# Mode rows in five kinds, turns rounded in bf16, and magnitude products issued twice

## The chip, the cores and the metric

One core of one Trainium2 chip runs the whole program. The metric is the device time of one execution in microseconds (us). The engines are named as the profile names them: PE is TensorE, PEld its weight loads, DVE is VectorE, ACT is ScalarE, POOL is GpSimd, SP is SyncE, which issues most DMAs.

## The reference

Four layers act on a 2048 x 512 sequence: A, B, A, B, each added to its input after a layer norm.

```
x = A_q
x = x + _A_ref(_layernorm(x), A_k, A_v, A_shift_k, A_ssm_k, A_ssm_D)
x = x + _B_ref(_layernorm(x), B_log_A_real, B_A_imag, B_C_real, B_C_imag, B_log_dt, B_D_skip)
(the same two lines again)

_A_ref: kv = (4-tap causal conv of k) * v;  q * (causal conv of kv with ssm_k + kv * ssm_D)
_B_ref: A = -exp(log_A_real) + i A_imag;  C = (C_real + i C_imag) * dt;  dt = exp(log_dt)
        P = exp(A * dt * pos)                       (512 channels, 128 modes, 2048 positions)
        K = 2 * Re(sum over modes of C * P);        causal conv of u with K, + u * D_skip
```

The part that the change touches makes K. For each channel and mode it needs a magnitude, exp(rate * n) with an offset log|C|, and an angle, rate * n with an offset arg C. Angles are counted in turns, and only their fraction matters for sine and cosine.

## The kernel before

The long convolutions are done by Fourier transforms built from matmuls, in chunks: `fwd_group` (L175, matmuls on L173, first step), `f2_chunk` (L195, matmul on L198, second step), a product with a spectrum on POOL and DVE (L285 to L288), and the way back (L297, L318). Constants of these steps are `wz`, `w2`, `mm`, `w4`.

The program has these stages. First, DVE, ACT and POOL prepare the mode numbers from the inputs (L342 to L433). The rates and offsets (four arrays of 128 x 512) go through `split` (L366), which cuts a float into three bf16 pieces: ACT copies to bf16 (L370, L372), POOL or DVE subtracts (L371, L373), and SP writes the pieces to a scratch array `rows_d` in DRAM (L374). Then two generators run side by side, one turn of the first to two of the second (`run_steps`):

- `stream`, with `taps` in it, makes K in 64 units of 8 channels, four units to a group `gi`. `load_rows` (L474) fetches a group's rows from DRAM into a tile `rw`, of which three exist. `mags` (L482) is a bf16 matmul of the rows with a table (`tg1` or `tg2`) into a PSUM bank, and then an exp on ACT (L492). `exps` does this for two groups at a time, 12 tiles, ahead of every eighth unit: a burst. `angles` (L497) multiplies rows with the table `tt` (L501), rounds the turns to a whole number `y` on DVE (L505) and subtracts it in PSUM with a second matmul by `minus`, the negated identity (L506). `waves` takes sine and cosine on ACT (L512 to L514), `products` multiplies with the magnitudes on POOL and DVE (L524 to L528), `contract` sums over the modes on PE (L538). All of `mags` and `angles` share three PSUM banks, tag `pa`.
- `diagonal` makes the spectrum of layer A's kernel (`spectrum_quarter`, L225; its tiles are `kk`, `pc`, `spec`) and the product kv (`gated`, L629), and then runs the first A convolution.

After that come the first gated update (L755), the B convolution, and both once more. A timeline planner orders the instructions of each engine ahead of time, by its own costs; on the chip every engine runs its list in order. So other instructions in `mags` and `angles` also change the order of the work around them.

In the kernel before, a row tile `rw` has 128 rows: two halves of 64 rows for two sets of 8 channels; each half has rates and offsets of 8 channels, in three pieces and a row of zeros. The tables `tt` and `tg1` are used with one half alone (the slice `hs`, 64 rows), `tg2` with all 128 rows. Turns reach some 1000, so `y` and `minus` are `F32R`, a float type for which the matmul loads its own weights: the program holds no separate weight load for it.

Of the kernel before, what the change touches and what calls it, by code (L numbers as in the profile page):

```python
# [79 lines left out]
def mode_constants():  # L80
    m = np.arange(32)
    n2 = np.concatenate([32 + m, 31 - m])
    tabs = {
        "tt": (8, np.concatenate([m + 1, 64 * m + 32]), np.repeat([0, 1], 32)),
        "tg1": (8, n2, 0 * n2),
        "tg2": (16, 64 * m, 0 * m + 1),
    }
    out = {}
    for name, (chans, rate, off) in tabs.items():
        t = np.zeros((2, 2, 8, 4, chans, len(rate)), np.float32)  # L90
        for s in range(2):
            for c in range(8):
                for r, factors in enumerate((rate, off)):
                    t[s, r, c, :3, (8 * s + c) % chans] = factors
        out[name] = t.reshape(128, chans, len(rate))
    out["minus"] = -np.eye(128, dtype=np.float32)
    return out

# [2 lines left out]
def kernel(ctx: ExitStack, tc: tile.TileContext, out, x_in, kv_in, ssmk_in, ssmd_in,  # L101
                           la_in, ai_in, cr_in, ci_in, ldt_in, ldtb_in, dsk_in,
                           w1_in, w2_in, mm_in, w4_in, minus_in, tt_in, tg1_in, tg2_in, dbg=None):
    nc = tc.nc
    V, S, G, T = nc.vector, nc.scalar, nc.gpsimd, nc.tensor
# [11 lines left out]
    kdram = [dram.tile([128, 512], F32, name=f"kdram{g}") for g in range(16)]  # L117
    ya_d = dram.tile([4, 128, 16, 128], F32, name="ya_d")
    kv_d = [dram.tile([128, 512], F32, name=f"kv_d{g}") for g in range(16)]
    rows_d = [dram.tile([NQ, 2, 128, 4, 128], BF16, name=f"rows_d{k}") for k in range(2)]  # L120

    cpool = sbuf(ctx, "cpool")
    GL = 2
# [230 lines left out]
    halfpi = gp.tile([128, 1], F32, name="halfpi")  # L354
    G.memset(halfpi, math.pi / 2)

    minus = gp.tile([128, 128], F32R, name="minus")
    G.dma_start(minus, minus_in)

    pieces = []  # L360
    for i in range(4):
        parts = nat.tile([128, 4, 4, 128], BF16, name=f"parts{i}")
        G.memset(parts[:, 3], 0.0)
        pieces.append(parts)

    def split(i, v, eng):  # L366
        k, r = divmod(i, 2)
        parts = pieces[i]
# [5 lines left out]
        nc.sync.dma_start(rows_d[k].rearrange("q h (s r c p) g n -> r (q h s) c (p g n)", s=2, r=2, p=4)[r],  # L374
                          parts.rearrange("p s g n -> p (s g n)"))

    bits = lambda t_: t_.bitcast(I32)
# [20 lines left out]
    split(2, la, G)  # L398
    y0 = nat.tile([128, 4, 128], F32, name="y0", tag="y0")
    V.tensor_scalar(y0, ai, MAGIC, MAGIC, op0=ALU.add, op1=ALU.subtract)  # L400
# [20 lines left out]
    V.tensor_mul(ph, ph, t0)  # L421
    V.scalar_tensor_tensor(ph, ph, -0.125, cr, op0=ALU.add, op1=ALU.mult)
# [44 lines left out]


    NR = 3
    rows, ms, pks, angs = {}, {}, {}, {}  # L470
    NM = 5
    last_exp, last_sin = [None], [None]

    def load_rows(gi):  # L474
        if gi in rows:
            return
        rows[gi] = wk.tile([128, 2, 2, 128], BF16, name="rw", tag="rw", bufs=NR)
        q, g = divmod(gi, 4)
        for k in range(2):
            nc.sync.dma_start(rows[gi][:, k], rows_d[k][q, :, :, g, :].rearrange("h x n -> x h n"))  # L480

    def mags(gi, k, col):  # L482
        h, s = divmod(k, 2)
        hs = slice(0, 128) if col == 2 else slice(64 * s, 64 * s + 64)
        pm = pp.tile([128, 512], F32, name="pm", tag="pa", bufs=NPA)
        T.matmul(pm, rows[gi][hs, 1, h, :], tabs["tg2" if col == 2 else "tg1"][hs], start=True, stop=True)  # L486
# [5 lines left out]
        i = S.activation(m, pm.rearrange("p (c i) -> p c i", c=16 if col == 2 else 8), AF.Exp)  # L492
        if last_sin[0] is not None:
            after(i, last_sin[0])
        last_exp[0] = i

    def angles(gi, k):  # L497
        h, s = divmod(k, 2)
        hs = slice(64 * s, 64 * s + 64)
        pa = pp.tile([128, 512], F32, name="pa", tag="pa", bufs=NPA)  # L500
        T.matmul(pa, rows[gi][hs, 0, h, :], tabs["tt"][hs], start=True, stop=False,  # L501
                 skip_group_check=True)

        y = wk.tile([128, 512], F32R, name="y", tag="y", bufs=2)
        V.tensor_scalar(y, pa, MAGIC, MAGIC, op0=ALU.add, op1=ALU.subtract)  # L505
        T.matmul(pa, minus, y, start=False, stop=True, skip_group_check=True)  # L506
        angs[gi, k] = pa
# [465 lines left out]
```

## Time and profile before

| what | value |
|---|---|
| median of three runs | 729.88 us (729.4 to 730.36) |
| profiled execution, its own time | 731.89 us |
| its span in the profile | 730.1 us |
| mean granted TensorE clock | 0.921 |
| PE busy | 587.1 us (80%) |
| DVE / ACT / POOL busy | 525.5 / 487.2 / 461.7 us |

The profiled execution took 2.0 us more than the median. In rows of the profile, `out<-in` are tile names, a form such as `64*128 64x512 bf16` is weights of 64 rows by 128 columns and moving data of 64 rows by 512 columns, and `[t <-X]` says that the engine was idle for t us until X released it. A float32 matmul stands as two instructions, so `x8` on L198 is one chunk of four matmuls, `x4` in an order row. "PEclk" is the share of full TensorE clock that was granted.

### The profile page before, as it was taken

The page shows a single profiled execution, that of the slowest core. Times are in us where ns is not written, and L with a number is a line of the kernel's source. Part 1 is how long each engine was busy: PE and PEld are TensorE (multiplying, and loading weights), DVE is VectorE, ACT ScalarE, POOL GpSimd, SP SyncE. Part 2 cuts the span into 40 slices and gives each one's busy share as a digit, 9 for nine tenths or more (in the row PEclk, how much of TensorE's full clock was granted, in tenths as well). Part 3 has the DMA queues.
Part 4 walks back from the last instruction along what each step waited for, and adds up shares of the span by engine and source line. Part 5 has one row for each costly group of instructions (what it writes and reads, how often), then busy time and mean ns, then how long its engine had stood idle before and what let it go on. Part 6 is the DMA issues. An engine that isn't in the chain of part 4 may idle for free.

```text
span 730.1 us, 14266 instructions
## 1 busy us (share of the span) xinstructions
PE 587.1 (80%) x4984; PEld 398.4 (55%) x4984; DVE 525.5 (72%) x947; ACT 487.2 (67%) x886; POOL 461.7 (63%) x483
## 2 busy tenths in 40 slices
PE   1376677589899999988998886988699808889996
PEld 0043444346576876665755464866377503666683
DVE  8836869868585874663565879566498898988875
ACT  3355566468779786785799667987457356696672
POOL 5535978859958695594596532077567502786783
PEclk9998999957999999998999898999899958999998
DMA  8556967766776477554473495668776250477772
GB/s 289 188 165 213 320 210 244 215 199 212 226 224 168 128 177 202 152 154 144 131 232 109 141 333 183 209 155 218 182 202 188 62 148 0 116 191 211 195 226 101
DMA packets 84555, 134.47 MB, mean 184 GB/s; under 512 B 16764, under 2 KB 33924, under 8 KB 83332
## 3 DMA queue, kind: packets, MB, share of 16 engines
q1 hardware_dynamic: 83268, 131.01, 60.8%
q0 software_dynamic: 1216, 2.56, 1.5%
q8 instruction: 39, 0.64, 0.4%
q14 instruction: 32, 0.26, 0.1%
HBM read 98.28 MB, written 35.65 MB: 183 GB/s over the span
## 4 chain that ended last, share of the span: by engine, by line
PE 31%; DVE 9%; ACT 9%; issue 5%; POOL 3%; DMA 3%; SPq 0%; DVEq 0%; POOLq 0%; ACTq 0%
PE pu L198 9%; PE pf L173 7%; PE po L318 6%; PE pi L297 6%; DMA kab<-spec 3%; ACT u L818 2%; DVE x L755 1%; POOL sw L287 1%; DVE w L312 1%; PE pk L538 1%; DVE x L832 1%; DVE vv L285 1%; ACT sw L283 1%; PE pm L486 1%; ACT sw L284 1%
## 5 line engine op out<-in xcount | busy, mean ns | idle before, releaser
L287 POOL TENSOR_TENSOR sw<-sw,kab 128x512 f32<-128x512 f32 x96 | 125.4, 1312 | 82.9 <-ACT sw L284 65.4
L285 DVE TENSOR_TENSOR vv<-pu,kab 128x512 f32<-128x512 f32 x96 | 65.1, 681 | 73.9 <-ACT sw L284 40.7
L297 PE MATMUL pi<-vv,mm 128*128 128x128 f32 x768 | 106.0, 283 | 9.3 <-DVE vv L285 6.7
L297 PEld LDWEIGHTS pi<-vv,mm 128*128 128x128 f32 x768 | 95.8, 195 | 21.6 <-issue 14.2
L288 POOL TENSOR_TENSOR vv<-vv,sw 128x512 f32<-128x512 f32 x76 | 98.9, 1304 | 7.8 <-DVE vv L285 5.3
L283 ACT ACTIVATE sw<-pu 64x512 f32<-64x512 f32 x96 | 57.1, 595 | 59.7 <-PE pu L198 56.4
L173 PE MATMUL pf<-kk,wz 128*128 128x256 f32 (+1 forms) x176 | 61.9, 599 | 39.3 <-issue 16.0
L636 POOL TENSOR_TENSOR term<-kvt 128x512 f32<-128x512 f32 x64 | 81.8, 1298 | 17.6 <-ACT acc L642 13.6
L198 PE MATMUL pu<-x,w 128*128 128x128 f32 x512 | 80.3, 304 | 13.1 <-ACT pc L249 9.0
L524 POOL TENSOR_TENSOR xye<-co,m 128x512 f32<-128x512 f32 x64 | 75.3, 1177 | 18.2 <-ACT co L514 9.0
L198 PEld LDWEIGHTS pu<-x,w 128*128 128x128 f32 x512 | 72.0, 212 | 27.2 <-ACT pc L249 10.1
L198 PEld LDWEIGHTS pu<-zu,w 128*128 128x128 f32 x512 | 62.7, 191 | 41.0 <-DVE vv L285 14.7
L198 PE MATMUL pu<-zu,w 128*128 128x128 f32 x512 | 72.6, 284 | 10.3 <-DVE vv L285 8.3
L173 PE MATMUL pf<-u,wz 128*128 128x256 f32 (+2 forms) x280 | 77.5, 493 | 3.7 <-DVE zu L191 2.5
L492 ACT ACTIVATE m<-pm 128x512 f32<-128x512 f32 x96 | 52.7, 612 | 18.3 <-PE pm L486 17.4
L318 PE MATMUL po<-w,w 128*64 128x512 f32 x192 | 57.2, 683 | 9.5 <-DVE w L312 8.2
L512 ACT ACTIVATE co<-pa 128x512 f32<-128x512 f32 x64 | 38.5, 601 | 38.0 <-PE pa L506 32.2
L249 ACT COPY pc<-pu 128x512 f32<-128x512 f32 x64 | 36.7, 586 | 39.1 <-PE pu L198 15.5
L173 PEld LDWEIGHTS pf<-kk,wz 128*128 128x128 f32 (+1 forms) x176 | 29.1, 220 | 55.4 <-issue 40.2
L538 PEld LDWEIGHTS pk<-xye 128*32 128x32 f32 x2048 | 36.8, 116 | 37.0 <-issue 18.4
L538 PE MATMUL pk<-xye 128*32 128x64 f32 x2048 | 51.6, 235 | 6.3 <-DVE ks L548 4.0
L284 ACT COPY sw<-pu 64x512 f32<-64x512 f32 x96 | 55.5, 578 | 1.1
(141 smaller groups left out, 1118.8 us busy)
## 6 DMA issues: line engine op xcount, KB each, us to landing
kab<-spec SPq DMA_DIRECT2D x188, 256.0 KB, 4.1
spec<-pc SPq DMA_DIRECT2D x64, 256.0 KB, 2.8
kvt<-kv_in SPq DMA_DIRECT2D x16, 624.0 KB, 5.8
yaq<-ya_d SPq DMA_DIRECT2D x5, 1024.0 KB, 8.6
kk<-ssmk_in SPq DMA_DIRECT2D x16, 256.0 KB, 4.8
kv_d<-un SPq DMA_DIRECT2D x16, 256.0 KB, 3.1
xt<-x_in SPq DMA_DIRECT2D x16, 256.0 KB, 4.3
kdram<-ks SPq DMA_DIRECT2D x64, 64.0 KB, 3.1
```

The lines of the kernel that those rows point to most:

```text
L173: yield T.matmul(o, w, rhs, start=True, stop=True)
L198: ins = T.matmul(pu[:, i, :], w2[:, c * CK + i, :], z[:, :, c * CK + i, :], start=True, stop=True)
L283: S.mul(sw[0:64], pu[64:128], -1.0)
L284: swapped[0] = S.copy(sw[64:128], pu[0:64])
L285: multiplied[0] = V.tensor_mul(vv, pu, kabs[s][:, 0])
L287: (V if last else G).tensor_mul(sw, sw, kabs[s][:, 1])
L288: (V if last or s % add_dve == add_dve - 1 else G).tensor_add(vv, vv, sw)
L297: i1s[t] = T.matmul(pi[:, i, :], mm[:, c * CK + i, :], vvs[t][:, i, :], start=True, stop=True)
L318: ins = T.matmul(po[64 * a:64 * a + 64], w4, ws[g][:, :, 16 * a:16 * a + 16, :].rearrange("p x t r -> p t x r"), start=True, stop=True, ti ...
L524: G.tensor_mul(xye[:, 0, :, 32:96], co[:, :, 1:65], m[:, :, 32:96])
L538: T.matmul(pk[32 * i4:32 * i4 + 32, 2 * k + i, :], xye[:, r, 4 * i + i4, 64:96], xye[:, r, 4 * i + i4, 0:64], start=r == 0, stop=r == 1, t ...
L636: G.tensor_mul(term, kvt[:, 3 - j:19 - j, :], tap(j))
```

## The change

Four things change, and L numbers after the change are given where order rows show them.

1. A fifth kind of row is made: `y0`, the fraction of 32 times the turns per step (three DVE instructions), which goes through `split` like the others. The table `tt` now is (m + 1) times the first fraction, (2m + 1) times the second, plus the offset. Turns stay below some 50, so that a whole number of turns is exact in bf16.
2. `y` and `minus` are bf16. Their matmul now has a weight load of its own.
3. A row tile holds five kinds x 8 channels x 3 pieces = 120 rows for each of the four units of a group, fetched by one DMA (two before). Every matmul of `mags` and `angles` uses all 120 rows. A `tg2` tile, one matmul of 512 columns before, takes two of 256.
4. In groups 0 to 5 (`WG = 6`) every product of `mags` is issued twice, with the same result.

```
+    tabs = {
+        "tt": {0: np.concatenate([m + 1, none]), 1: np.concatenate([none, 2 * m + 1]),
+               2: np.repeat([0, 1], 32)},
+        "tg1": {3: n2},
+        "tg2": {3: 64 * m, 4: none + 1},
+    }
...
-    rows_d = [dram.tile([NQ, 2, 128, 4, 128], BF16, name=f"rows_d{k}") for k in range(2)]
+    rows_d = dram.tile([16, 5, 8, 3, 4, 128], BF16, name="rows_d")
...
-    minus = gp.tile([128, 128], F32R, name="minus")
+    minus = gp.tile([128, 128], BF16, name="minus")
...
-        parts = nat.tile([128, 4, 4, 128], BF16, name=f"parts{i}")
-        G.memset(parts[:, 3], 0.0)
...
+        parts = nat.tile([128, 3, 4, 128], BF16, name=f"parts{kind}")
...
+    V.tensor_scalar(y0, ai, 32.0, MAGIC, op0=ALU.mult, op1=ALU.add)
+    V.tensor_scalar(y0, y0, MAGIC, None, op0=ALU.subtract)
+    V.scalar_tensor_tensor(y0, ai, 32.0, y0, op0=ALU.mult, op1=ALU.subtract)
+    split(1, y0, G)
...
-        rows[gi] = wk.tile([128, 2, 2, 128], BF16, name="rw", tag="rw", bufs=NR)
-        for k in range(2):
-            nc.sync.dma_start(rows[gi][:, k], rows_d[k][q, :, :, g, :].rearrange("h x n -> x h n"))
+        rows[gi] = wk.tile([120, 4, 128], BF16, name="rw", tag="rw", bufs=NR)
+        nc.sync.dma_start(rows[gi], rows_d[4 * q:4 * q + 4, :, :, :, g, :].rearrange("k a c p n -> (a c p) k n"))
...
-        T.matmul(pm, rows[gi][hs, 1, h, :], tabs["tg2" if col == 2 else "tg1"][hs], start=True, stop=True)
+        if col == 2:
+            for i in (0, 1, 0, 1)[:4 if gi < WG else 2]:
+                T.matmul(pm[:, 256 * i:256 * i + 256], rows[gi][:, k + i, :], tabs["tg2"], start=True, stop=True)
+        else:
+            for _ in range(2 if gi < WG else 1):
+                T.matmul(pm, rows[gi][:, k, :], tabs["tg1"], start=True, stop=True)
...
-        T.matmul(pa, rows[gi][hs, 0, h, :], tabs["tt"][hs], start=True, stop=False,
+        T.matmul(pa, rows[gi][:, k, :], tabs["tt"], start=True, stop=False, skip_group_check=True)
...
-        y = wk.tile([128, 512], F32R, name="y", tag="y", bufs=2)
+        y = wk.tile([128, 512], BF16, name="y", tag="y", bufs=2)
```

The order moves at three places that matter below. The first is the start of PE's list, before the change (`tg_217` is the table `tg2`, `tg_219` is `tg1`, `w_104` is `w2`, `x` a spectrum tile):

```order
L173 MATMUL pf<-kk,wz 128x16x16x2 x8
L486 LDWEIGHTS rw
L486 MATMUL pm<-tg_217,rw 128x512
L486 LDWEIGHTS rw
L486 MATMUL pm<-tg_219,rw 128x512
L486 LDWEIGHTS rw
L486 MATMUL pm<-tg_219,rw 128x512
L198 MATMUL pu<-x,w_104 128x128 x8
```

And the same place after it (`tg_222` is `tg2`, `tg_224` is `tg1`; L174, L199, L485 and L488 are the lines L173, L198 and L486 of before):

```order
L174 MATMUL pf<-kk,wz 128x16x16x2 x8
L199 MATMUL pu<-x,w_103 128x128 x8
L174 MATMUL pf<-kk,wz 128x16x16x2 x2
L485 LDWEIGHTS rw
L485 MATMUL pm<-tg_222,rw 128x256
L485 LDWEIGHTS rw
L485 MATMUL pm<-tg_222,rw 128x256
L485 LDWEIGHTS rw
L485 MATMUL pm<-tg_222,rw 128x256
L485 LDWEIGHTS rw
L485 MATMUL pm<-tg_222,rw 128x256
L488 LDWEIGHTS rw
```

Two chunks of the A spectrum (L198, 8 matmuls) and a transform step now stand ahead of the first magnitudes, which are four short products where one long one stood.

The second place is DVE's list at the end of the preparation, before the change (`t_151` is log|C|, `parts` the pieces that are written to DRAM):

```order
L418 TENSOR_TENSOR t_151<-t_151,t_150 128x512
L422 SCALAR_TENSOR_TENSOR ph<-ph,cr 128x512
L423 SCALAR_TENSOR_TENSOR ph<-ph,ci 128x512
L191 STREAM_TRANSPOSE x<-pf 128x512 x2
L371 TENSOR_TENSOR rest<-ph,parts_143 128x512
L373 TENSOR_TENSOR parts_143<-rest,parts_143 128x512
L371 TENSOR_TENSOR rest<-t_151,parts_147 128x512
L373 TENSOR_TENSOR parts_147<-rest,parts_147 128x512
```

And after it (L398 to L400 are the new fraction, L192 is L191 of before, L365 and L367 are L371 and L373):

```order
L398 TENSOR_SCALAR y_168<-ai 128x512
L416 TENSOR_TENSOR t_142<-t_142,t_141 128x512
L420 SCALAR_TENSOR_TENSOR ph<-ph,cr 128x512
L399 TENSOR_SCALAR y_168<-y_168 128x512
L192 STREAM_TRANSPOSE x<-pf 128x512 x2
L421 SCALAR_TENSOR_TENSOR ph<-ph,ci 128x512
L400 SCALAR_TENSOR_TENSOR y_168<-ai,y_168 128x512
L365 TENSOR_TENSOR rest<-ph,parts_207 128x512
L192 STREAM_TRANSPOSE x<-pf 128x512 x2
L367 TENSOR_TENSOR parts_207<-rest,parts_207 128x512
L365 TENSOR_TENSOR rest<-t_142,parts_214 128x512
L367 TENSOR_TENSOR parts_214<-rest,parts_214 128x512
```

Three more instructions and a second pair of transposes now stand ahead of the last pieces.

The third place is PE's list in the stretch where taps, spectrum and A convolution run together, before the change:

```order
L297 MATMUL pi<-vv,mm 128x128 x4
L173 MATMUL pf<-u,wz 128x16x8x2 x4
L506 MATMUL pa<-y,minus 128x512 x2
L173 MATMUL pf<-kk,wz 128x16x8x2 x4
L198 MATMUL pu<-x,w_104 128x128 x4
L297 MATMUL pi<-vv,mm 128x128 x4
L506 MATMUL pa<-y,minus 128x512
L173 MATMUL pf<-u,wz 128x16x8x2 x2
```

And after it (L298 and L505 are L297 and L506 of before):

```order
L298 MATMUL pi<-vv,mm 128x128 x4
L174 MATMUL pf<-u,wz 128x16x8x2 x4
L505 LDWEIGHTS minus
L505 MATMUL pa<-y,minus 128x512
L505 LDWEIGHTS minus
L505 MATMUL pa<-y,minus 128x512
L174 MATMUL pf<-kk,wz 128x16x8x2 x4
L199 MATMUL pu<-x,w_103 128x128 x4
L298 MATMUL pi<-vv,mm 128x128 x4
L505 LDWEIGHTS minus
L505 MATMUL pa<-y,minus 128x512
L174 MATMUL pf<-u,wz 128x16x8x2 x2
```

The order is the same here; each subtraction of whole turns now has a weight load ahead of it.

More of the change, by code (lines that the diff above doesn't have):

```diff
@@ L82, in mode_constants @@
     n2 = np.concatenate([32 + m, 31 - m])
+    none = 0 * m
     tabs = {
-        "tt": (8, np.concatenate([m + 1, 64 * m + 32]), np.repeat([0, 1], 32)),
-        "tg1": (8, n2, 0 * n2),
-        "tg2": (16, 64 * m, 0 * m + 1),
+        "tt": {0: np.concatenate([m + 1, none]), 1: np.concatenate([none, 2 * m + 1]),
+               2: np.repeat([0, 1], 32)},
+        "tg1": {3: n2},
+        "tg2": {3: 64 * m, 4: none + 1},
     }
     out = {}
-    for name, (chans, rate, off) in tabs.items():
-        t = np.zeros((2, 2, 8, 4, chans, len(rate)), np.float32)
-        for s in range(2):
+    for name, kinds in tabs.items():
+        t = np.zeros((5, 8, 3, 8, len(kinds[max(kinds)])), np.float32)
+        for kind, factors in kinds.items():
             for c in range(8):
-                for r, factors in enumerate((rate, off)):
-                    t[s, r, c, :3, (8 * s + c) % chans] = factors
-        out[name] = t.reshape(128, chans, len(rate))
+                t[kind, c, :, c] = factors
+        out[name] = t.reshape(120, 8, -1)
     out["minus"] = -np.eye(128, dtype=np.float32)
@@ L355, with split @@
     G.memset(halfpi, math.pi / 2)
-    minus = gp.tile([128, 128], F32R, name="minus")
+    minus = gp.tile([128, 128], BF16, name="minus")
     G.dma_start(minus, minus_in)
-    pieces = []
-    for i in range(4):
-        parts = nat.tile([128, 4, 4, 128], BF16, name=f"parts{i}")
-        G.memset(parts[:, 3], 0.0)
[L364 to L368, printed above, removed]
+    def split(kind, v, eng):
+        parts = nat.tile([128, 3, 4, 128], BF16, name=f"parts{kind}")
         rest = nat.tile([128, 4, 128], F32, name="rest", tag="rest", bufs=2)
@@ L373, in split @@
         eng.tensor_sub(parts[:, 2], rest, parts[:, 1])
-        nc.sync.dma_start(rows_d[k].rearrange("q h (s r c p) g n -> r (q h s) c (p g n)", s=2, r=2, p=4)[r],
+        nc.sync.dma_start(rows_d[:, kind].rearrange("a c p g n -> a c (p g n)"),
                           parts.rearrange("p s g n -> p (s g n)"))
@@ L397 @@
     G.tensor_mul(la, la, across(dtn))
-    split(2, la, G)
+    split(3, la, G)
     y0 = nat.tile([128, 4, 128], F32, name="y0", tag="y0")
@@ L423 @@
     V.scalar_tensor_tensor(ph, ph, 0.25, ci, op0=ALU.add, op1=ALU.mult)
-    split(1, ph, V)
-    split(3, t2, V)
+    split(2, ph, V)
+    split(4, t2, V)
     S.activation(warm, t2[:, 0, 0:1], AF.Exp, scale=0.0)
     tabs = {}
-    for key, c_, w_, src in (("tg2", 16, 32, tg2_in), ("tg1", 8, 64, tg1_in), ("tt", 8, 64, tt_in)):
-        tabs[key] = gp.tile([128, c_, w_], BF16, name=key)
+    for key, w_, src in (("tg2", 32, tg2_in), ("tg1", 64, tg1_in), ("tt", 64, tt_in)):
+        tabs[key] = gp.tile([120, 8, w_], BF16, name=key)
         G.dma_start(tabs[key], src)
@@ L469 @@
     NR = 3
+    WG = 6
     rows, ms, pks, angs = {}, {}, {}, {}
@@ L476, in load_rows @@
             return
-        rows[gi] = wk.tile([128, 2, 2, 128], BF16, name="rw", tag="rw", bufs=NR)
+        rows[gi] = wk.tile([120, 4, 128], BF16, name="rw", tag="rw", bufs=NR)
         q, g = divmod(gi, 4)
-        for k in range(2):
-            nc.sync.dma_start(rows[gi][:, k], rows_d[k][q, :, :, g, :].rearrange("h x n -> x h n"))
+        nc.sync.dma_start(rows[gi], rows_d[4 * q:4 * q + 4, :, :, :, g, :].rearrange("k a c p n -> (a c p) k n"))
     def mags(gi, k, col):
         h, s = divmod(k, 2)
-        hs = slice(0, 128) if col == 2 else slice(64 * s, 64 * s + 64)
         pm = pp.tile([128, 512], F32, name="pm", tag="pa", bufs=NPA)
-        T.matmul(pm, rows[gi][hs, 1, h, :], tabs["tg2" if col == 2 else "tg1"][hs], start=True, stop=True)
+        if col == 2:
[4 more added lines that the diff above has]
+                T.matmul(pm, rows[gi][:, k, :], tabs["tg1"], start=True, stop=True)
         if col == 2:
@@ L497, in angles @@
     def angles(gi, k):
-        h, s = divmod(k, 2)
-        hs = slice(64 * s, 64 * s + 64)
         pa = pp.tile([128, 512], F32, name="pa", tag="pa", bufs=NPA)
-        T.matmul(pa, rows[gi][hs, 0, h, :], tabs["tt"][hs], start=True, stop=False,
-                 skip_group_check=True)
-        y = wk.tile([128, 512], F32R, name="y", tag="y", bufs=2)
+        T.matmul(pa, rows[gi][:, k, :], tabs["tt"], start=True, stop=False, skip_group_check=True)
+        y = wk.tile([128, 512], BF16, name="y", tag="y", bufs=2)
         V.tensor_scalar(y, pa, MAGIC, MAGIC, op0=ALU.add, op1=ALU.subtract)
```

## Prediction

> **What bounds the kernel now.** I read the page first for the balance of the engines, then the busy time by stage, then PE's instructions in order of time where the clock is low.
>
> ```profile
> span 730.1 us, 14266 instructions
> PE 587.1 (80%) x4984; PEld 398.4 (55%) x4984; DVE 525.5 (72%) x947; ACT 487.2 (67%) x886; POOL 461.7 (63%) x483
> core 0: us, PE busy (x) PEld busy (x) DVE busy (x) ACT busy (x) POOL busy (x), PEclk, DMA share, GB/s
> 41.00:59.00 18.00, 15.48 (x75) 9.33 (x75) 8.74 (x14) 10.29 (x19) 8.18 (x9) 1.00 0.59 193
> 59.00:65.90 6.90, 5.41 (x16) 3.49 (x17) 2.65 (x6) 1.74 (x3) 2.69 (x3) 0.51 0.17 47
> 65.90:144.40 78.50, 53.77 (x648) 32.59 (x646) 64.06 (x123) 46.31 (x82) 64.97 (x68) 0.93 0.79 254
> 144.40:158.00 13.60, 11.52 (x84) 6.24 (x85) 7.26 (x18) 8.36 (x14) 7.94 (x10) 0.50 0.84 259
> 158.00:161.40 3.40, 2.69 (x14) 0.81 (x14) 3.04 (x6) 3.04 (x6) 1.29 (x2) 1.00 0.26 91
> 161.40:171.70 10.30, 9.74 (x27) 5.49 (x25) 7.69 (x14) 8.29 (x15) 9.75 (x10) 0.50 0.72 232
> 171.70:225.00 53.30, 47.78 (x645) 34.64 (x644) 40.74 (x74) 42.49 (x77) 42.66 (x47) 1.00 0.66 201
> 225.00:300.00 75.00, 72.73 (x718) 52.78 (x718) 47.31 (x79) 58.20 (x100) 53.98 (x57) 1.00 0.66 171
> 300.00:425.00 125.00, 110.80 (x1200) 73.67 (x1198) 75.99 (x123) 95.86 (x167) 82.48 (x83) 0.92 0.55 158
> ```
>
> PE is the fullest engine, but not everywhere. From 65.9 to 144.4 it works 53.8 of 78.5 us; DVE, POOL and the transfers (0.79, 254 GB/s) are ahead of it, so PE work there has room. From 144.4 to 171.7 PE is nearly always busy, at half clock for two stretches of 13.6 and 10.3 us. From 225 to 300 it is 97% busy at full clock: there more PE work is more time. From 300 to 425 it has gaps again. After 425 the changed code hardly runs, and I take that part as only shifted.
>
> ```profile
> 145.47 2.08 PE L198 MATMUL pu<-x,w 128*128 128x128 f32 x8 [2.97 <-ACT pc L249]
> 150.68 2.07 PE L173 MATMUL pf<-kk,wz 64*128 64x512 f32 x2
> 152.68 1.15 PE L486 MATMUL pm<-tg,rw 128*128 128x512 bf16 x3
> 163.68 2.08 PE L198 MATMUL pu<-x,w 128*128 128x128 f32 x8
> 172.18 1.16 PE L198 MATMUL pu<-x,w 128*128 128x128 f32 x8
> 602.72 10.01 PE L767 MATMUL idle<-x,wz 128*128 128x512 f32 x16 [17.19 <-issue]
> 601.80:608.60 6.80, 5.88 (x7) 2.52 (x8) 6.80 (x22) 5.48 (x14) 0.00 (x0) 0.50 0.00 0
> 608.60:612.00 3.40, 3.40 (x9) 1.52 (x8) 2.99 (x22) 2.51 (x8) 0.50 (x1) 1.00 0.01 2
> ```
>
> The same chunk of L198 takes 2.08 us at half clock and 1.16 at full. What brings the clock back is not being busy alone. The idle matmuls of L767, full 128 x 128 weights, restored it after 5.88 us of work. In the low stretch, 11.52 busy us bring it back for one step of 3.4 us, and it falls again; there the transforms (L173) and most magnitude products fill 64 of the 128 rows.
>
> **The change part by part.** Sums are against the profiled execution's 731.9 us, which stands 2.0 above the median of 729.9; 2.0 comes off at the end.
>
> *Start.*
>
> ```profile
> 41.01 1.15 PE L486 MATMUL pm<-tg,rw 128*128 128x512 bf16 x3 [4.15 <-DMA rw<-rows_d]
> 42.09 3.60 PE L198 MATMUL pu<-x,w 128*128 128x128 f32 x16
> 60.49 2.08 PE L198 MATMUL pu<-x,w 128*128 128x128 f32 x8 [4.00 <-ACT pc L249]
> L400 DVE TENSOR_SCALAR y<-ai 128x512 f32<-128x512 f32 x1 | 0.4, 413 | 0.0
> L422 DVE SCALAR_TENSOR_TENSOR ph<-ph,cr 128x512 f32<-128x512 f32 x1 | 1.8, 1751 | 0.0
> L191 DVE STREAM_TRANSPOSE x<-pf 128x512 f32<-128x512 f32 x32 | 20.9, 690 | 5.8 <-PE pf L173 5.8
> ```
>
> The first magnitudes wait 4.15 us for their rows, and 3.60 us of transform work waits behind them. DVE gets two instructions like L400 (0.41 each), one like L422 (at most 1.75, priced at 1.2) and two transposes (0.69 each) ahead of the last pieces: 3.4 us. The last write is three quarters as large, which I put at 1 us back, so rows come some 2.3 us later. But the two chunks now run inside the wait, so PE's list starts about 2.8 us earlier and is not idle. The first burst gets 4.6 us longer (next part): PE is 1.9 us late at 56. There it waits 4.00 us for a copy that waits for a transfer, which takes up the 1.9. Net 0, between -2.8 and +4.6. The extra casts on ACT and two subtractions on POOL lie beside the DVE work; four POOL memsets and one row DMA of each group go, and no engine waits on those.
>
> *Doubled and split products.* The price of a bf16 product with its load, from a pair:
>
> ```profile
> 229.68 0.71 PE L486 MATMUL pm<-tg,rw 128*128 128x512 bf16 x2
> 230.32 0.94 PE L198 MATMUL pu<-x,w 128*128 128x128 f32 x6
> L486 PEld LDWEIGHTS <-rw 128*128 128x128 bf16 x20 | 2.0, 98 | 3.4 <-issue 2.8
> ```
>
> Two take 0.64, so 0.32 each; 0.10 of it is the load, 0.22 streaming. One of 256 columns is then 0.10 + 0.11 = 0.21. A group had 6 products, 1.92 us; a doubled one has 8 x 0.21 + 8 x 0.32 = 4.24. A burst of two groups is 4.6 us longer at full clock. Three bursts are doubled: the first is counted above; the second lies near 100 us, where PE has room (0, at most 4.6); the third in the low stretch, where PE is idle for 3.3 of 27.3 us. I let 1.5 of it vanish there and take +3.1.
>
> *Clock.* Full rows and doubled products are the kind of work that L767 shows to restore the clock. From 150.7 on, PE is at half clock and busy for 7.3 + 9.7 = 17.0 us; at full clock this saves 1 - 1.16 / 2.08 = 44%, or 7.5. The stretch at 59 to 65.9 (5.41 busy, worth 2.4) may close too, since the idle time ahead of it shrinks; I take half. Together -8.7, between -9.9 and 0.
>
> *Turns in bf16.* DVE's rounding reads the same PSUM bank and writes fewer bytes; I price it the same, 0.67. The product by `minus` on PE:
>
> ```profile
> 240.12 1.89 PE L173 MATMUL pf<-u,wz 128*128 128x256 f32 x8
> 241.66 0.82 PE L506 MATMUL pa<-y,minus 128*128 128x512 f32 x2
> 244.04 0.39 PE L198 MATMUL pu<-x,w 128*128 128x128 f32 x2
> 246.06 1.03 PE L173 MATMUL pf<-u,wz 128*128 128x256 f32 x4
> 247.02 0.39 PE L501 MATMUL pa<-tt,rw 64*128 64x512 bf16 x1
> 247.34 1.13 PE L173 MATMUL pf<-u,wz 128*128 128x256 f32 x4
> 248.40 0.39 PE L501 MATMUL pa<-tt,rw 64*128 64x512 bf16 x1
> L506 PEld LDWEIGHTS pa<-y,minus 128*128 128x128 f32 x45 | 8.2, 193 | 9.7 <-DVE y L505 7.0 <-DVE xye L526 0.8 <-issue 0.5
>   DVE y L505: 10.3, 12
> by line: issue 12.5%; PE pu L198 11.4%; PE pf L173 11.1%; PE po L318 6.5%; PE pi L297 5.8%; PE pk L538 4.9%; ACT m L492 4.2%; ACT co L512 4.0%; ACT co L514 3.5%; PE pm L486 3.5%; ACT x L298 3.1%; ACT L513 3.1%; DVE w L312 3.0%; POOL xye L52
> ```
>
> From 240.12 to 244.04 run sixteen L173 and two L506. Eight L173 without a neighbour take 1.73 (0.216 each), so the two L506 cost 3.92 - 3.46 = 0.46, or 0.23 each: their loads are hidden. From 246.06 to 248.40 eight L173 and one bf16 product take 2.34, 0.61 more; 0.10 of it is the next product's load. A lone bf16 product among float32 ones costs 0.51: its load and the load behind it both show. So the bf16 form is dearer by 0.28 alone, and by 0.09 beside another bf16 product (0.32). In the last 40 units the new order has 13 alone and 27 beside one: 3.6 + 2.4. Twenty split `tg2` tiles add 0.10 each, 2.1 in all: 8.1 us of PE work from 172 to 425. PE's share of the path there lies between the 97% busy up to 300 and the 43% that its lines have in the chain of waits after (the last row); 0.7 gives 5.7. Against it, 12 loads of `minus` waited for `y` in this stretch; a separate load need not, and saves 0.19 each on a path on which PE is awaited: -2.3. Net +3.4, between -2.8 and +8.1.
>
> Sum: 0 + 3.1 - 8.7 + 3.4 = -2.2; 731.9 - 2.2 - 2.0 = 727.7.
>
> **The rivals.**
>
> *The turns are paid in full.* The stretch up to 300 leaves no room, and the waits saved are none, because what ends last there is DVE. Then 8.1 stands for 3.4: 732.4. For it: 72.73 of 75.00 busy. Against it: PE idles 14 us from 300 to 425.
>
> *The low clock stays* (the slower side). PE reaches the third burst after a wait like the 2.97 us at 145.47, the clock drops, and work at half clock is too thin to restore it. Then -8.7 is lost and the burst costs 9.2 for 3.1: 742.5. It is decided by whether PE's idle time just ahead of the third burst stays over 3 us, and by whether the doubled products then restore the clock at all. The Trainium skill, "TensorE: Matmul & The Clock Gate", section "What's actually happening", has the array at full clock after one window of some 3.4 us in which PE was busy. By that rule alone fuller rows would change nothing, as PE was busy already, and this rival would hold; the 11.52 busy us at 0.50 speak against busy time as the whole measure, and I leave it a chance.
>
> *Loads run ahead.* If the load of `minus`, which never changes, slips under the matmul before it, a bf16 product costs 0.22, no more than the 0.23 of now, and the waits saved stay: -2.8 instead of +3.4, 721.5. The Trainium skill, same page, section "Step-by-step: what each phase is for", says that weight loads are pulled ahead of matmuls in flight where row groups differ or the spare weight buffer is free. Against it: rows of full and half height alike show 0.32 per bf16 product here, load and stream one after the other.
>
> *Transfers set the pace up to 172.* Clock and doubling are both hidden there: 731.9 + 3.4 - 2.0 = 733.3. For it: 0.79 to 0.84 DMA share. Against it: PE is busy without gaps from 150.7.
>
> **How the numbers follow.** A change under 0.2% (728.4 to 731.3) can't be told from none here. My forecast, 727.7, has a chance of 0.43, its own range 724 to 731 (faster 0.33, same 0.10). Turns in full 0.20 (slower 0.15, same 0.05), low clock 0.12 (slower), loads ahead 0.10 (faster), transfers 0.15 (slower 0.11, same 0.04). That makes faster 0.43, same 0.19, slower 0.38. The range 719 to 738 takes in all cases but the low clock, and the ends of the unknown terms.
>
> **What would show it.** Right: a PEclk of 0.8 or more between 140 and 175; PE already at work on L199 before 41 us; the chunk of L198 that starts at 172.18 starting some 5 us earlier. L505 products at 0.5 us among float32 ones, and PE over 97% busy from 220 to 300, would show the price of bf16. Wrong: half clock through the third burst, or a start of the first magnitudes later than 45 us with PE idle before it; or bf16 products at a pitch of 0.22.

## The result and the profile after

| | before | after |
|---|---|---|
| median of four runs beside each other | 729.64 us (722.87 to 730.36) | 705.85 us (699.70 to 707.13) |
| ratio, 95% interval | 1 | 0.9677 (0.9597 to 0.9758) |
| profiled execution, its span, granted clock | 731.89, 730.1 us, 0.921 | 707.13, 705.4 us, 0.939 |

The kernel is 3.2% faster. The forecast was 727.7 us with a range of 719 to 738: the sign was right, the size was not, and the time lies 13 us below the range. A run that took over 1.5% longer than the fastest of its kernel is left out of every ratio here and below, so a ratio is not always that of the medians beside it. Line numbers of the changed kernel are one more than before in the transforms (L199 is L198 of before) and one less in the products and behind them (L537 is L538, L641 is L642, L754 is L755); the exp of the magnitudes is L494, L492 before.

The busy line of the page after, with the same columns as before:

```profile
span 705.4 us, 14397 instructions
PE 574.8 (81%) x5060; PEld 401.1 (57%) x5064; DVE 523.1 (74%) x950; ACT 487.8 (69%) x888; POOL 460.3 (65%) x481
```

PE has 76 instructions more and is busy 12.3 us less. The busy time by stage, after, in the stretches that the prediction used:

```profile
core 0: us, PE busy (x) PEld busy (x) DVE busy (x) ACT busy (x) POOL busy (x), PEclk, DMA share, GB/s
59.00:65.90 6.90, 4.30 (x14) 1.53 (x15) 6.90 (x13) 4.90 (x8) 6.45 (x6) 0.83 0.97 339
65.90:144.40 78.50, 63.14 (x721) 36.98 (x724) 65.56 (x130) 49.37 (x87) 64.71 (x71) 0.85 0.76 253
144.40:158.00 13.60, 11.34 (x86) 6.86 (x79) 9.62 (x17) 9.38 (x17) 9.49 (x10) 0.96 0.67 223
161.40:171.70 10.30, 8.32 (x111) 6.35 (x111) 9.32 (x19) 8.39 (x17) 10.30 (x12) 1.00 0.62 193
225.00:300.00 75.00, 71.70 (x761) 56.92 (x762) 53.35 (x90) 61.93 (x108) 57.56 (x61) 1.00 0.66 178
```

Around 150 and 165 us PE is at full clock now, as forecast. But the same work stands some 12 us earlier, and two shorter stretches at half clock stand ahead of it:

```profile
128.40:135.20 6.80, 6.19 (x98) 4.34 (x87) 3.74 (x10) 2.38 (x6) 4.28 (x4) 0.50 0.95 300
138.60:145.50 6.90, 6.90 (x36) 2.75 (x34) 3.69 (x8) 4.05 (x8) 5.71 (x8) 0.51 0.81 266
```

So the low clock is shorter, not gone: from 41 to 225 us the granted clock is 0.89 before and 0.92 after. In the second of these stretches PE is busy throughout, and ten of its instructions are magnitude products on 120 rows, yet the clock stays at half. From 225 to 300 PE does 761 instructions in 71.70 us where it did 718 in 72.73. The mix differs a little (268 of the 128-column float32 instructions of L199 and L298 for 214, 80 of the 256-column ones of L174 for 96), but it is more work in less time, which the prediction's price of a bf16 product excludes.

Where the time came from is read off three landmarks. First, the last products of the fourth unit on PE, before and then after:

```profile
86.67 0.65 PE L538 MATMUL pk<-xye 128*32 128x64 f32 x32 [0.38 <-POOL xye L528]
```

```profile
75.17 0.65 PE L537 MATMUL pk<-xye 128*32 128x64 f32 x32
```

Then the way back of the convolutions (L297 before, L298 after) and the first and last gated update, before and after (count, shortest, median and longest in ns, then first and last start):

```profile
L297 PE MATMUL pi<-vv,mm x768: 269/275/580, 222.3 to 717.7; 128*128 128x128 f32 x192
L755 DVE SCALAR_TENSOR_TENSOR x<-x,nm,ut x32: 708/734/2261, 430.6 to 608.6; 128x512 f32<-128x512 f32 x32
```

```profile
L298 PE MATMUL pi<-vv,mm x768: 269/275/421, 210.1 to 693.4; 128*128 128x128 f32 x192
L754 DVE SCALAR_TENSOR_TENSOR x<-x,nm,ut x32: 722/737/760, 407.5 to 584.2; 128x512 f32<-128x512 f32 x32
```

The changed kernel is 11.5 us ahead at 76 us, 12.2 at the first matmul of the way back in the A convolution, 23.1 at the first gated update and 24.4 at the last. So half is won ahead of 76 us, where the prediction's sum has 0, and half between 210 and 410, where it has +3.4 for the turns.

The first half is seen on ACT. Its list around 41 us, before and then after (`m` is an exp of the first magnitudes, `pc` a copy of a spectrum chunk, the first `acc` starts the chain of kv):

```profile
41.66 1.62 ACT L492 ACTIVATE m<-pm 128x512 f32<-128x512 f32 x3 [8.92 <-PE pm L486]
44.20 0.59 ACT L249 COPY pc<-pu 128x512 f32<-128x512 f32 x1 [0.92 <-PE pu L198]
...
46.40 0.59 ACT L642 COPY acc<-term 128x512 f32<-128x512 f32 x1
```

```profile
38.17 0.58 ACT L250 COPY pc<-pu 128x512 f32<-128x512 f32 x1 [4.12 <-PE pu L199]
...
40.47 0.59 ACT L641 COPY acc<-term 128x512 f32<-128x512 f32 x1
41.66 1.58 ACT L494 ACTIVATE m<-pm 128x512 f32<-128x512 f32 x3 [0.61 <-PE pm L485]
```

Before, ACT stood 8.92 us at the first exp, whose rows were on their way, and behind it in its list stood copies that were ready. After, these copies go first: the kv chain starts at 40.47 and not 46.40, the first spectrum copy at 38.17 and not 44.20. The first exps run at 41.66 in both.

### The profile page after: what moved, and what is told of

It reads as the page before. It is cut to its first block, busy times and chain, and to the rows that moved or that the text cites. A ratio compares the mean times of both kernels' runs of the same rounds, so it can differ in the third digit from the quotient of the medians.

```text
span 705.4 us, 14397 instructions
## 1 busy us (share of the span) xinstructions
PE 574.8 (81%) x5060; PEld 401.1 (57%) x5064; DVE 523.1 (74%) x950; ACT 487.8 (69%) x888; POOL 460.3 (65%) x481
## 5 line engine op out<-in xcount | busy, mean ns | idle before, releaser
L298 PE MATMUL pi<-vv,mm 128*128 128x128 f32 x768 | 106.6, 284 | 3.6 <-DVE vv L286 2.5
L298 PEld LDWEIGHTS pi<-vv,mm 128*128 128x128 f32 x768 | 98.0, 198 | 17.0 <-issue 7.0
L174 PE MATMUL pf<-kk,wz 128*128 128x256 f32 (+1 forms) x176 | 58.9, 580 | 38.8 <-issue 21.2
L523 POOL TENSOR_TENSOR xye<-co,m 128x512 f32<-128x512 f32 x64 | 75.5, 1179 | 22.1 <-ACT co L513 12.8
L635 POOL TENSOR_TENSOR term<-kvt 128x512 f32<-128x512 f32 x64 | 81.5, 1291 | 12.3 <-ACT acc L641 9.8
L199 PEld LDWEIGHTS pu<-zu,w 128*128 128x128 f32 x512 | 66.0, 199 | 40.8 <-DVE vv L286 14.9
L199 PEld LDWEIGHTS pu<-x,w 128*128 128x128 f32 x512 | 70.9, 207 | 28.1 <-ACT pc L250 12.1
L199 PE MATMUL pu<-x,w 128*128 128x128 f32 x512 | 77.1, 296 | 11.5 <-ACT pc L250 8.0
L199 PE MATMUL pu<-zu,w 128*128 128x128 f32 x512 | 76.1, 293 | 9.8 <-DVE vv L286 8.9
L174 PE MATMUL pf<-u,wz 128*128 128x256 f32 (+2 forms) x280 | 76.2, 477 | 4.3 <-DVE zu L192 2.5
L319 PE MATMUL po<-w,w 128*64 128x512 f32 x192 | 53.7, 634 | 9.1 <-DVE w L313 8.1
L174 PEld LDWEIGHTS pf<-kk,wz 128*128 128x128 f32 (+1 forms) x176 | 28.0, 211 | 56.9 <-issue 28.1
L494 ACT ACTIVATE m<-pm 128x512 f32<-128x512 f32 x96 | 52.8, 608 | 10.9 <-PE pm L485 7.0
L537 PEld LDWEIGHTS pk<-xye 128*32 128x32 f32 x2048 | 36.2, 116 | 36.4 <-issue 18.6
L524 DVE TENSOR_TENSOR xye<-pa,m 128x512 f32<-128x512 f32 x64 | 43.3, 676 | 16.8 <-ACT pa L512 8.3
```

The lines of the kernel that those rows point to most:

```text
L174: yield T.matmul(o, w, rhs, start=True, stop=True)
L199: ins = T.matmul(pu[:, i, :], w2[:, c * CK + i, :], z[:, :, c * CK + i, :], start=True, stop=True)
L298: i1s[t] = T.matmul(pi[:, i, :], mm[:, c * CK + i, :], vvs[t][:, i, :], start=True, stop=True)
L319: ins = T.matmul(po[64 * a:64 * a + 64], w4, ws[g][:, :, 16 * a:16 * a + 16, :].rearrange("p x t r -> p t x r"), start=True, stop=True, ti ...
L523: G.tensor_mul(xye[:, 0, :, 32:96], co[:, :, 1:65], m[:, :, 32:96])
L635: G.tensor_mul(term, kvt[:, 3 - j:19 - j, :], tap(j))
```

## Experiments

Four theories were tried. *Order*: each edit makes the planner write another order of all engines, and this order is the gain. *Start*: the order up to 76 us alone. *Loads*: products on full rows hide their weight loads. *Clock*: fuller, doubled products hold the clock. Each ratio is against the kernel before in the same session (medians 729.66 to 731.41 us), with its 95% interval.

### One edit at a time, the planner free

```
a_nodup  -    WG = 6                              +    WG = 0
a_mag56  -  rows[gi][:, k + i, :], tabs["tg2"]    +  rows[gi][64:120, k + i, :], tabs["tg2"][64:120]
            (and the same for tg1)
a_f32r   -  minus, y in BF16                      +  minus, y in F32R
b_full   (on before) tg1, tt: [128, 8, 64]        +  [128, 16, 64], half s zero outside its 64 rows
         -  rows[gi][hs, ...], tabs[...][hs]      +  rows[gi][:, ...], tabs[...][:, 8 * s:8 * s + 8]
```

> The changed kernel with WG = 0: no magnitude product is issued twice. Three theories stand. Loads: the gain comes from bf16 products that now fill 120 rows, whose weight loads run under the matmul before, where 64-row products showed theirs and the next one. Start: the gain of the first 80 us comes from the new order of work there. Clock: the doubled, fuller products keep the granted clock up. Loads and Start expect no loss without the doubling, 703 to 708 us. Clock expects the half-clock stretches at 59 to 66 and 144 to 172 to come back, worth 2.4 + 7.5 us: 713 to 717 us, with a mean clock near 0.92.

> The changed kernel, but the magnitude products use rows 64 to 119 alone (the other rows of their tables are zeros, so the values are the same): 56-row weights, the counts and the doubling unchanged. Loads: each product again shows its load of 0.10 us and slows the load behind it by about as much. Some 80 such products stand in the stretch after 225 us, where PE is the bound, so 8 to 16 us are lost: 714 to 722 us, with a product-to-product pitch of 0.31 to 0.32 us for 512 columns instead of 0.216. Clock: thin rows let the clock fall in the doubled bursts, 7 us lost: 713 us, with the pitch at full clock unchanged. Start: no change, 704 to 708 us.

> The changed kernel with the whole turns and the negated identity back in F32R, so the matmul by it loads its own weights again. Loads: the F32R product already had its load hidden (0.23 us each before), so the bf16 form saves nothing on PE; only the load's wait for y comes back, 12 such waits of 0.19 us: 705 to 709 us. The prediction's price (bf16 dearer by 8.1 us of PE work, 2.3 us of waits saved) would make this kernel 3 us faster than the changed one, 702 to 703 us. If the bf16 form were where the gain came from, 715 us or more.

> The kernel before, with one thing changed: the tables tg1 and tt stand twice, each copy zero in the other half's rows, so that every product of mags and angles uses all 128 rows. Counts, values, rows and doubling as before. Loads: 64 + 64 products lose their shown load and that behind it, 0.1 to 0.2 us each; some 80 of them lie in the stretch after 225 us where PE is the bound: 8 to 16 us gained, 714 to 722 us, with the pitch of L501 products to float32 ones falling from 0.31 to 0.22 us. Start: nothing, 727 to 732 us, unless the order at the start moves too. Clock: if the rows that weights fill hold the clock, the low stretches at 144 to 172 us close, 722 us, with the gain there and not after 225.

| kernel | median us | ratio to before |
|---|---|---|
| a_nodup | 719.05 | 0.9893 (0.9816 to 0.9970) |
| a_mag56 | 729.40 | 1.0024 (0.9978 to 1.0071) |
| a_f32r | 721.13 | 0.9924 (0.9877 to 0.9972) |
| b_full | 727.43 | 0.9971 (0.9920 to 1.0022) |

Taken at face value, each of the first three edits undoes more than half of the gain, which sums to far more than there is. The times of a_nodup and a_mag56 lie outside every range that was expected. Each of the four also came with another order on every engine: by the traces, some 900 to 1700 of PE's 5000 matmul instructions stand elsewhere in its list. These runs change two things at a time and decide little. The granted clock does not decide on Clock either: it is 0.936 to 0.938 in the four runs of a_nodup and 0.939 to 0.956 in those of the changed kernel, lower by some 0.01, with another order. Against Loads as the whole gain, b_full's products reached a pitch of 0.22 us among float32 ones, as expected, and its time hardly moved.

### The order held fixed

So the order was written out. Each instruction is chained behind the one that stands ahead of it on its engine in a chosen plan. The chain by itself costs nothing that shows: the changed kernel takes 704.93 us with it (r_after) and 705.85 without.

```
+def replay(nc, tc):          # rank: each instruction's place in the chosen plan
...
+    for r, i in sorted(((r, k) for k, r in enumerate(rank) if r < 65535)):
+        i = ins[i]
+        if i.engine in last:
+            tc.add_manual_dep(i, last[i.engine].name, ...NoSync..., reason="order")
+        last[i.engine] = i
```

> The changed kernel with its own planned order written out as a fixed order: on each engine every instruction is chained behind the one that stood ahead of it. This is the same program and the base for the runs with a fixed order: 704 to 708 us by every theory.

> The instructions of the kernel before (64-row products, F32R turns, no doubling, its row loads) in the fixed order that the planner made for the changed kernel. Theory Order: each edit makes the planner write another order of all engines, and that order, not the edited instructions, is the gain: 705 to 712 us. Theory Loads: the full-row products with hidden loads are the gain, and the order is neutral: 722 us or more, with 0.31 us pitches of the 64-row products back. Theory Clock: as Loads, with the half-clock stretch at 144 to 172 us back.

> The instructions of the changed kernel in the fixed order of the kernel before (the three new instructions for the second fraction and its pieces are left for the planner to place, row loads stand where the second of the two stood). Order: no gain, or a loss for the 4 to 8 us of added PE work: 728 to 736 us. Loads: most of the gain of 24 us is there, 705 to 715 us, 12 us of it between 230 and 425 us. Both in part: 715 to 724 us.

> The changed kernel without the second issue of the magnitude products, in the fixed order that the planner made for the changed kernel. When the planner was free, leaving them out cost 13 us (719.05). Order: that loss was another plan, and here the time is that of the changed kernel or 1 to 4 us less, 701 to 707 us. Clock: the doubled products themselves hold the clock, and the loss stays: 714 to 720 us, with more time at half clock before 180 us.

| instructions of | order of before | order of after |
|---|---|---|
| before | 1 | 0.9771 (0.9701 to 0.9840), 712.12 us |
| after | 0.9959 (0.9927 to 0.9991), 727.71 us | 0.9651 (0.9592 to 0.9711), 704.93 us |

after without doubling, order of after: 0.9650 (0.9585 to 0.9715), 703.98 us.

The old instructions in the new order have 16.7 us of the gain (0.0229 of 730); the new instructions in the old order have 3.0. The rest, some 6 us, would need both, but it is not clear of the intervals, which reach up to 5 us to either side. The gated update starts at 411.6 us with old instructions in the new order and at 433.1 with new instructions in the old:

```profile
L755 DVE SCALAR_TENSOR_TENSOR x<-x,nm,ut x32: 707/733/1541, 411.6 to 585.4; 128x512 f32<-128x512 f32 x32
```

```profile
L754 DVE SCALAR_TENSOR_TENSOR x<-x,nm,ut x32: 709/734/862, 433.1 to 607.1; 128x512 f32<-128x512 f32 x32
```

The doubling is worth nothing that shows: 703.98 against 704.93 us, the two intervals alike. The 13 us that a_nodup lost were its other plan. The clock does answer to the doubling. From 130 to 182 us, with the order of after, doubled and not doubled, and then doubled in the order of before:

```profile
130.00:182.00 52.00, 41.41 (x493) 26.44 (x491) 37.51 (x69) 39.60 (x70) 44.52 (x47) 0.93 0.71 232
```

```profile
130.00:182.00 52.00, 42.18 (x410) 26.18 (x399) 34.66 (x68) 35.04 (x61) 41.97 (x42) 0.75 0.65 216
```

```profile
130.00:182.00 52.00, 41.99 (x359) 24.83 (x360) 35.52 (x71) 29.28 (x51) 34.92 (x36) 0.74 0.66 211
```

The granted clock (the column of 0.93, 0.75 and 0.74) is high only with both. A profile is one execution, though, and the changed kernel's first profile has 0.85 there with the same order and instructions as the 0.93. Taken from 41 to 225 us, the clock sorts the profiles in the order of after all the same: 0.92 to 0.95 in the four with doubled products on 120 rows (the changed kernel twice, oa_f32r and oa_tt72 of below), 0.89 without the doubling, 0.88 with doubled products on 56 rows (oa_mag56 of below), 0.83 with the instructions of before. The time does not follow: the one with 0.83 gains 16.7 us over the kernel before, which has 0.89, and without the doubling the median is much the same. What the clock term is worth stays open below some 6 us, the width of the intervals.

### Which part of the order, and which part of the products

h_4 and h_32 follow the order of after up to the last product of the 4th and the 32nd unit, and the order of before from there on. oa_f32r and oa_mag56 are a_f32r and a_mag56 with the order of after held.

> The changed kernel's instructions, all engines in the changed kernel's order up to the last product of the fourth unit (some 76 us) and in the order of the kernel before from there on. With the order of before throughout, these instructions took 727.7 us and finished that unit at 92.4 us; with their own order throughout 704.9 us, at 76.8. If the start alone decides, the 15 us stay: 711 to 716 us. If the middle takes the start's gain back as room elsewhere, 722 to 728 us.

> As the last, with the changed kernel's order up to the last product of the 32nd unit (some 220 us), then the order of before. Own order reached that point at 217.5 to 221 us, the order of before at 241. If the gain is made up to there, 704 to 710 us; if the order after it matters as much, 712 to 718 us.

> The changed kernel with the turns back in F32R, in the fixed order of the changed kernel. Pitches at full clock in the runs so far: into the bf16 product by minus 0.110 us behind a 128-column float32 matmul and 0.216 out of it; for F32R 0.028 in and 0.318 out. That is 0.33 against 0.35 us, and 0.22 against 0.34 beside another: 45 such products where PE is full cost 1 to 4 us more in F32R: 705 to 709 us. By the prediction's price (bf16 dearer by 0.09 to 0.28 each), 699 to 703 us. The 721 us with a free planner would be its other order.

> The changed kernel with magnitude products on rows 64 to 119 alone, in the fixed order of the changed kernel. Their loads show again at each change between these rows and full ones: 0.20 for 0.11 us into a run of them, 0.31 for 0.22 out. Some 25 to 40 such runs stand after 220 us: Loads expects 4 to 8 us more than the changed kernel, 708 to 714 us. Clock: thin rows also let the clock fall ahead of 180 us, 712 to 720 us. If loads and rows do not matter where order is fixed, 703 to 707 us. The 729 us with a free planner would be its other order.

| kernel | median us | ratio to before |
|---|---|---|
| h_4 | 715.73 | 0.9799 (0.9742 to 0.9856) |
| h_32 | 713.06 | 0.9738 (0.9687 to 0.9789) |
| oa_f32r | 709.10 | 0.9710 (0.9650 to 0.9769) |
| oa_mag56 | 713.83 | 0.9749 (0.9690 to 0.9808) |

The order up to 76 us keeps 12 of the 23 us that lie between 727.71 and 704.93. From there to 220 us the order adds no more than the intervals allow (2.7 us); the order after 220 us adds 8 by the medians and 6 by the ratios, whose intervals just overlap. The traces bear it out. From the first matmul of the way back to the first gated update pass 192.7 to 197.4 us in all seven profiles in the order of after, whatever their products, and 202.5 to 208.3 in the six that follow the order of before there (before, ob_after, h_4, h_32, and h_m and b_swap of below).

F32R turns cost 4.2 us more than bf16 ones by the medians, with overlapping intervals; the prediction had them cheaper, and no run shows that. Thin rows (oa_mag56) cost 8.9 us, which Loads (708 to 714 us) and Clock (712 to 720) both allowed. With the planner free, these two edits read as 15 and 24 us.

The price of rows shows on PE. One 56-row product between float32 ones (oa_mag56), then one of 128 rows (after):

```profile
216.71 1.06 PE L199 MATMUL pu<-x,w 128*128 128x128 f32 x8
217.70 0.39 PE L488 MATMUL pm<-tg,rw 56*128 56x512 bf16 x1
218.01 1.16 PE L298 MATMUL pi<-vv,mm 128*128 128x128 f32 x8
```

```profile
232.60 1.05 PE L298 MATMUL pi<-vv,mm 128*128 128x128 f32 x8
233.49 0.38 PE L505 MATMUL pa<-y,minus 128*128 128x512 bf16 x1
233.70 1.03 PE L174 MATMUL pf<-u,wz 128*128 128x256 f32 x4
```

Eight float32 instructions and the product take 1.30 us (216.71 to 218.01) with 56 rows, 1.10 (232.60 to 233.70) with all: 0.10 us is lost ahead of the product and 0.10 behind it. A third 0.10 follows: the eight L298 behind the 56-row product take 1.16 us, and 1.05 in the second view. So one product of few rows between full-row float32 ones costs 0.30 us more than one of all rows. Beside the contraction (L538 before, weights of 32 columns) the rows make no difference: 0.15 us into a product and 0.31 out of it, with 64 rows before as with 120 after.

That is the price on PE. How much of the 8.9 us of oa_mag56 it is stays open. Loads expected them after 220 us, but most of them stand ahead of the first L298 (at 215.7 us, where two profiles of the changed kernel have 210.1 and 206.7), where its clock is lower too.

### The first 44 us, one move, full rows alone, and 72 rows

b_swap is the kernel before in its own order with one move; ob_full is b_full, oa_tt72 the changed kernel with `rows[gi][0:72, k, :], tabs["tt"][0:72]` in `angles`, each in the held order of its own base; h_m follows after up to the third exp of the first magnitudes, then before.

```
b_swap   PE:   - L486 pm x3, L198 pu x16       + L198 pu x16, L486 pm x3
         ACT:  - L492 m x3, L249 pc x2         + L249 pc x2, L492 m x3
```

> The changed kernel's instructions, in the changed kernel's order only up to the third exp of the first magnitudes (some 44 us), and in the order of the kernel before from there on. The order up to the fourth unit kept 12 us of the gain (715.7 against 727.7 us). If what stands ahead of the first magnitudes decides (two chunks and their copies on ACT, and the first copy of the kv chain), 8 to 12 us are kept: 715 to 720 us. If it is the order between 44 and 76 us, 723 to 728 us.

> The kernel before in its own fixed order, with one thing moved: on PE the first two chunks of the A spectrum ahead of the first three magnitude products, on ACT their two copies ahead of the first three exps. The copy that starts the kv chain stays behind the exps. If filling the wait is what counts, the chain on ACT starts 3 us earlier and 2 to 5 us are gained: 725 to 728 us. If it is the kv chain behind the exps, or more of the order, nothing: 729 to 732 us.

> The kernel before with all magnitude and angle products on 128 rows (tables doubled, the other half zero), in the fixed order of the kernel before. Full rows alone: loads hidden at some 80 products after 220 us, 0.1 to 0.2 us each, if PE ends the waits there: 718 to 724 us. If the order of before lets DVE and ACT end the waits there, as the 2.6 us between the two sets of instructions in that order suggest: 726 to 730 us. The start can lose 1 us to the tables, which are 64 KB to 128 KB larger.

> The changed kernel in its own fixed order, with the angle products on rows 0 to 71 alone (the other rows of that table are zeros). If any product with fewer rows than its neighbours shows its load, 64 such products lose 0.1 to 0.2 us each, half of them where PE is full: 708 to 714 us, with 0.20 us into and 0.31 out of such a product. If only a product that fits in 64 rows does, as the 56-row and 64-row ones did, the pitches stay at 0.11 and 0.22 us: 703 to 707 us.

| kernel | median us | ratio to before |
|---|---|---|
| h_m | 720.47 | 0.9860 (0.9761 to 0.9958) |
| b_swap | 724.20 | 0.9908 (0.9859 to 0.9958) |
| ob_full | 726.29 | 0.9923 (0.9870 to 0.9976) |
| oa_tt72 | 704.98 | 0.9645 (0.9579 to 0.9711) |

h_m keeps 7 of the 12 us by the medians, with a wide interval. Its trace says more. The last products of the fourth unit, all with the instructions of after, in the order of before (ob_after), in h_m, and in the order of after (r_after):

```profile
91.73 0.65 PE L537 MATMUL pk<-xye 128*32 128x64 f32 x32
```

```profile
78.89 0.65 PE L537 MATMUL pk<-xye 128*32 128x64 f32 x32
```

```profile
76.18 0.65 PE L537 MATMUL pk<-xye 128*32 128x64 f32 x32
```

There h_m has 12.8 of the 15.6 us: most of the start's gain is decided by the order up to 44 us. At the first matmul of the way back h_m and h_4 are 0.9 us apart (211.9 and 211.0). The rest of their difference arises behind it, where both follow the order of before.

The move of two chunks by itself makes the kernel before faster, by 0.4 to 1.4%. Its ACT list:

```profile
40.25 0.58 ACT L249 COPY pc<-pu 128x512 f32<-128x512 f32 x1 [7.66 <-PE pu L198]
41.96 0.58 ACT L249 COPY pc<-pu 128x512 f32<-128x512 f32 x1 [1.12 <-PE pu L198]
42.44 1.58 ACT L492 ACTIVATE m<-pm 128x512 f32<-128x512 f32 x3
43.88 0.63 ACT L642 COPY acc<-term 128x512 f32<-128x512 f32 x1
```

The kv chain starts 2.5 us earlier (43.88 against 46.40). Its first gated update also starts 2.5 us earlier, at 428.1 us. That much is shown as the move; the rest of its 6.7 us by the ratio arises behind that, in code that nothing changed, where the clock of that profile was higher (0.95 against 0.92 from 430 to 720 us), and I do not count it. Full rows alone in the old order gain 0.2 to 1.3%, so the products do gain something without the new order. oa_tt72 costs nothing, and its rows show no load:

```profile
249.24 1.05 PE L298 MATMUL pi<-vv,mm 128*128 128x128 f32 x8
250.13 0.38 PE L501 MATMUL pa<-tt,rw 72*128 72x512 bf16 x1
250.35 1.06 PE L199 MATMUL pu<-x,w 128*128 128x128 f32 x8
```

Eight float32 instructions and the product take 1.11 us, as with all rows, and the eight behind it 1.06. So not fewer rows as such show the load, but 56 or 64 of them. The Trainium skill, "TensorEngine Tiling (Array Packing)", has two lines that fit: section "When to Use Tiling" gives a contraction of at most 64 rows the half-height mode, and section "Key Properties" says that changing the mode drains the array. The 0.30 us of the 56-row product against none at 72 rows agrees with that.

No version was found that beats the changed kernel: without the doubling (703.98 us) and with 72-row angle products (704.98 us) it takes the same time.

## Why the prediction was wrong

**Start, 0 forecast, 12 us gained.** The step that failed is "Net 0", worked out from "PE's list starts about 2.8 us earlier": it followed PE alone. PE does run the two chunks inside the wait, as forecast:

```profile
36.06 3.75 PE L199 MATMUL pu<-x,w 128*128 128x128 f32 x16 [2.72 <-DVE x L192]
40.97 0.61 PE L485 MATMUL pm<-tg,rw 120*128 120x256 bf16 x4
```

The rows were put 2.3 us too late: the first magnitudes start at 40.97 us, where they started at 41.01. DVE's last piece starts 1.3 us later and not 3.4, before and then after:

```profile
32.77 0.69 DVE L373 TENSOR_TENSOR parts<-rest,parts 128x512 bf16<-128x512 f32 x1 [0.68 <-ACT parts L372]
```

```profile
34.09 0.69 DVE L367 TENSOR_TENSOR parts<-rest,parts 128x512 bf16<-128x512 f32 x1 [0.68 <-ACT parts L366]
```

What the sum left out is that the wait for rows also held ACT, 8.92 us, with the copies of the chunks and the start of the kv chain behind it, and the order now lets these pass. The prediction named the two chunks and not their two copies on ACT; it should have asked for each engine what stands behind the first instruction that waits for the rows. b_swap shows 2.5 us for two chunks and two copies; h_4 shows 12 for the whole order up to 76 us, and h_m's trace puts most of that ahead of 44 us. Which of the other moves make it was not tried. The one that the rows show is the copy that starts the kv chain: it goes ahead of the first exps in the order of after and stayed behind them in b_swap.

**The order after 76 us, not in the sum at all.** "The order is the same here" was read from 8 rows at one place. h_4 against the changed kernel shows 10.8 us in what follows, some 6 to 8 of them after 220 us (h_32). Which moves make them was not tried.

**Turns in bf16 and split products, +3.4 forecast.** The sign was wrong. 0.32 us for a bf16 product was read from a pair at 229.68 that the prediction's row gives as `128*128 ... x2`. The forms of that pair, before, line L486 from 229 to 230.4 us:

```profile
L486 PE MATMUL pm<-tg,rw x2: 387/388/390, 229.7 to 230.0; 128*128 128x512 bf16 x1, 64*128 64x512 bf16 x1
```

A grouped row names the form of its first instruction only. The pair was one product of 128 rows and one of 64, so it held a change of rows, which "Against it: rows of full and half height alike show 0.32" overlooked. The 0.51 of the lone L501 is right for a product of 64 rows, 0.22 and the 0.30 of above. But full-row products between float32 ones go at 0.22 us, and the split ones of 256 columns at 0.11: the price was of what the change removes, not of what it adds. The 8.1 us of added PE work do not exist, and oa_f32r finds the bf16 turns no dearer than F32R.

**The rival "Loads run ahead" had the mechanism and the wrong reach.** It let the load of `minus` alone slip under the matmul before, for -2.8 us. All bf16 products on full rows do that between full-row float32 ones. With the order of after, all new instructions against the old ones are worth 7.2 us by the medians (712.12 to 704.93; the intervals just overlap), and full rows alone in the old order 5.6 us by the ratio of ob_full (2 to 9 by its interval). Of the signs that the prediction named for being wrong, this one came: bf16 products at a pitch of 0.22.

**Doubling, +3.1, and clock, -8.7.** The doubled products cost no time that shows. The clock came back in part. From 41 to 225 us it is 0.89 before, and 0.92 and 0.94 in two profiles of the changed kernel; had the three low stretches of the prediction's rows (30.8 us) closed, it would be some 0.97, by an estimate from these rows. The sign "a PEclk of 0.8 or more between 140 and 175" came, 0.92, in part because the low stretch had moved ahead of it. From the fourth unit to the first matmul of the way back, where the sum has +3.1 - 8.7 = -5.6, the two profiles gain 0.7 and 5.1 us. So the size of the two terms stays open; the held order shows no difference in time with and without the doubling, within 6 us.

**DVE's rounding** was priced the same, 0.67 us, and is: 42.1 us for 64 in both.

## What to carry to other kernels

Where a planner orders the instructions, one edit is two changes; hold the order fixed before giving the time to the edit, or the plan's luck is read as the edit's price (13 us for a doubling that shows no cost when the order is held). At a wait for data look at every in-order engine that touches it, and at what is ready behind the waiting instruction there. Give a product of 64 rows or fewer full rows with zeros in its table if it stands alone among full-row float32 matmuls: here that is worth 0.30 us each.

## What was not expected of the hardware

Two products of different 64-row halves run at the same time. Three angle products around 55.8 us, before with 64 rows and after with 120:

```profile
55.89 0.60 PE L501 MATMUL pa<-tt,rw 64*128 64x512 bf16 x3
```

```profile
55.80 0.82 PE L501 MATMUL pa<-tt,rw 120*128 120x512 bf16 x3
```

With halves, three take 0.60 us, one product's streaming (0.22) less than with 120 rows: the first two start together, 4 ns apart in the trace. So half rows are not only a cost. Where both halves are issued back to back they save a product's time, and where one stands between full-row float32 matmuls it costs 0.30 us; the kernel before had both. The Trainium skill, "TensorEngine Tiling (Array Packing)", section "Key Properties", says that different tiles of the array work in parallel, and these rows agree.
